# Where four query transposes and four residual tiles are asked for, in a two-block linear-attention and gated-MLP kernel

## The chip, the cores and the metric

The kernel runs on one core of a Trainium2 chip. The metric is the device time of one execution in microseconds (us). The engines are TensorE (PE in the profile, with PEld for its weight loads), VectorE (DVE), ScalarE (ACT), GpSimd (POOL) and SyncE (SP). SP computes nothing here; it issues most of the DMAs, in the order of its queue.

## The reference, cut to what matters

The input `x` has 2048 rows of 1024 numbers. Four layers follow one another, each on the normalised rows and each added to `x`:

```
x = x + A(layernorm(x)); x = x + B(layernorm(x))
x = x + A(layernorm(x)); x = x + B(layernorm(x))

A:  q, k, v = split(x @ wqkv)          # 32 heads of 32
    pq, pk  = phi(q), phi(k)           # phi(t) = t + 1 if t > 0 else exp(t), + 1e-6
    kv = sum_s pk v ;  z = sum_s pk
    o  = (pq @ kv) / (pq . z + 1e-6) ;  return o @ wo
B:  gate, up = x @ W_gate, x @ W_up    # 1024 -> 3584
    return (relu(gate) * up) @ W_down
```

## The kernel before, in words

Rows are held as 16 tiles of 128 rows (`t` = 0 to 15); four tiles make a quarter. The residual lives in SBUF as 16 tiles `x[t]`. Layers 0 and 2 are attention layers (`layer_A`), layers 1 and 3 gated layers (`layer_B`).

**Attention layer, its end.** The queries of a tile, `pq`, are multiplied with the key sums on POOL (`z_mult`, L616), summed on DVE (`z_sum`, L621 to L623), scaled on POOL (`z_scale`, L628), and turned by a DMA transpose that SP issues (L633) into `pqT` of their quarter. The attention's output is then a product of `pqT` with a folded weight `T` (`out_unit`, L659), two units for each tile, added to the residual on DVE (L670 for tiles 0 to 7, L674 for tiles 8 to 15). Quarters 0, 1 and 2 go through `out_unit`. The last quarter (`sc` = 3, tiles 12 to 15) does not: its output is made later, inside the next gated layer, by `out_pairs`, a Strassen-like scheme that first forms sums of `T` (`sums_T`, DVE L505, and in layer 0 also ACT copies of the residual, L697), then sums of `pqT[3]` (`sums_q`, DVE L505), then seven products (L727) that are added to `x[12]` to `x[15]` (L720).

The residual tiles are not kept whole in SBUF in that stretch: in layer 0 they are loaded again from the input (`load_x`, L415, 256 KB each), in layer 2 brought back from a spill (`bring_back`, L256, 512 KB each). `behind(last_turn, ...)` queues these loads on SP behind the last transpose of queries issued so far.

**Gated layer, its start.** Tiles are normalised on ACT and DVE into `xnb` and turned by SP's DMA transposes (`ln_turn`, L378) into `xnT`. For each of the first four pairs of tiles DVE forms four sums (`sums_x`, L893 to L896) into the tiles `s`. A gated unit (`glu`) is 14 products of four matmuls each (L920). The first unit begins with four products that read `xnT` of the first quarter only (`xg`, `xu`, twice), then goes to products that read `s` (`vg`, `vu`, `yg` and so on), for which all four `sums_x` of the chunk are needed. Weights of the units come through a ring of five buffers: `ring.load_to` at the beginning of a unit asks for those of the units ahead (L844 and, where precomputed sums are read back, L847).

**What sets the order.** Work that accompanies the products is handed to a list of due times: `later.at(n, f)` calls `f` after `n` ticks, and every product unit makes one tick. One out unit is one tick, one product of a gated unit is one tick. Inside the attention layer's end DVE and POOL keep exactly the order in which the program asks; the other engines and all of the gated layer are ordered by the framework's planner, which goes by program order and its own costs. All 8 KB-per-partition buffers (weights, `pq`, `pqT`, `xnT`, `s`, and others) share one pool of 16; a new one takes a buffer that has been given back.

The due times around the change, counted from where `run(row_major(out_unit, 1))` starts: `z_scale` of tile 12 is due at tick 3, of 13 at 6, of 14 at 9, of 15 at 12. Residual tiles 8 and 9 are asked for at tick 2, 10 and 11 at 4, 12 and 13 at 6, 14 and 15 at 8. The transposes of `xnT` tiles 4 to 7 are due at 5, 7, 9, 11, `sums_x` at 11, 13, 15 and 16. The first gated unit begins after tick 16.

Of the kernel before, what the change touches and what calls it, by code (L numbers as in the profile page):

```python
# [14 lines left out]
P = 128  # L15
NW = 512
HD = 32
QT = 4
# [71 lines left out]
class _Net:  # L90
# [337 lines left out]
    def layer_A(self, l, last_ln):  # L428
        nc, G, KT, D = self.nc, self.G, self.KT, self.D
        ring, later = self.ring, self.later  # L430
        H = D // NW
        heads = lambda a: a.rearrange("p (h d) -> p h d", d=HD)
        pq_of, pqT, T = {}, {}, []
# [180 lines left out]
        def z_mult(sc, j):  # L614
            prod = ksum
            nc.gpsimd.tensor_tensor(out=prod, in0=pq_of[sc, j], in1=zrow, op=ALU.mult)  # L616
            later.at(2, lambda: z_sum(prod, sc, j))

        def z_sum(prod, sc, j):
            den = self.small.tile([P, D // HD], F32, tag="den")  # L620
            nc.vector.tensor_reduce(out=den, in_=heads(prod), axis=mybir.AxisListType.X, op=ALU.add)  # L621
            nc.vector.tensor_scalar(out=den, in0=den, scalar1=1e-6 * self.mean, scalar2=None, op0=ALU.add)
            nc.vector.reciprocal(out=den, in_=den)  # L623
            later.at(2, lambda: z_scale(den, sc, j))

        def z_scale(den, sc, j):
            pq = pq_of[sc, j]
            nc.gpsimd.tensor_tensor(  # L628
                out=heads(pq), in0=heads(pq),
                in1=den[:, :].unsqueeze(2).to_broadcast([P, D // HD, HD]), op=ALU.mult)  # L630
            if sc not in pqT:
                pqT[sc] = self.slot(f"pqT{l}_{sc}")
            self.last_turn = nc.sync.dma_start_transpose(out=pqT[sc][:, :, j * P:(j + 1) * P], in_=pq)  # L633

        def fold_wo(n):

            n2, a = divmod(n, H)
            if n2 == 0:
                T.append(self.slot(f"T{l}_{a}", [P, 4, D]))
            ps = [pool.tile([P, NW], F32, tag=tag, name=f"fold{l}_{n}_{i}") for i, (pool, tag) in  # L640
                  enumerate(((self.kvp, "kv0"), (self.kvp, "kv1"), (self.ps3, "b"), (self.ps3, "b")))]
            wo = ring.get((l, f"o{n2}"))
            for b in range(R):
                g = a * R + b
                for i in range(R):
                    e = slice(i * HD, (i + 1) * HD)
                    nc.tensor.matmul(ps[i][b * HD:(b + 1) * HD, :], lhsT=kvT[e, g, e],
                                     rhs=wo[e, g, :], start=True, stop=True,
                                     tile_position=(i * HD, b * HD))
            for i in range(R):  # L650
                g = a * R + i
                dst = T[g // 4][:, g % 4, n2 * NW:(n2 + 1) * NW]
                nc.scalar.activation(out=dst, in_=ps[i], func=ACT.Copy)
# [84 lines left out]
        def column_major(f, q):  # L738
            return [lambda j=j, c=c: f(q, j, c) for c in range(H) for j in range(QT)]

        def row_major(f, q):
            return [lambda j=j, c=c: f(q, j, c) for j in range(QT) for c in range(H)]

        def run(*lists):

            n = max(len(u) for u in lists)
            for i in range(n):
                for u in lists:
                    if i < len(u):
                        u[i]()  # L750
                        later.tick()
# [32 lines left out]
        with self.tc.manual_schedule(engines={mybir.EngineType.DVE, mybir.EngineType.Pool}):  # L784
            q3 = row_major(q_unit, self.NQ - 1)
            out0 = column_major(out_unit, 0)
            bring = self.bring_back if l else self.load_x
            ring.load_to(ring.index((l, "v1")) + 1)
            m_products(q3.pop(0))
            q3.insert(0, lambda: None)  # L790
            later.at(1, lambda: self.behind(ring.last, bring, range(self.NS)))
            for t in range(self.NS, self.ST, 2):
                later.at(10 + t, lambda t=t: self.behind(self.last_turn, bring, (t, t + 1)))

            def with_fold(u, i):
                return lambda: (u(), fold_wo(i // 2) if i % 2 == 0 else None)

            run(q3[:2])
            run([with_fold(u, i) for i, u in enumerate(q3[2:] + out0[:1])])
            run(out0[1:3])  # L800
            ring.free_slowly((l, "o0"), later, 2)
            for i in range(11, self.ST):
                later.at(1 + 3 * (i - 11), lambda i=i: z_mult(*divmod(i, QT)))
            self.ln_later(last_ln, 0, 2, 2, 2)
            run(out0[3:])
            for sc in range(1, self.NQ - 1):
                if sc == 1:
                    for j in range(QT):
                        self.ln_at(2 * j + 2, last_ln, QT + j, 2)
                        later.at((11, 13, 15, 16)[j], lambda j=j: self.sums_x(last_ln, 0, j))  # L810
                if sc == 2 and l == 0:
                    for n, w in enumerate("gu"):
                        later.at(2 + 2 * n, lambda w=w: self.make_gu(ring.get((last_ln, 0, w, 0)), w, 0))
                run(row_major(out_unit, sc))
            self.pairs = out_pairs(self.NQ - 1)
# [343 lines left out]
```

## Time and profile before

| what | value |
|---|---|
| median of 4 runs | 1472.87 us |
| the runs | 1474.16, 1471.57, 1474.73, 1471.00 us |
| profiled execution, its own time | 1474.16 us |
| its span in the profile | 1472.4 us |
| mean granted TensorE clock | 0.999 |
| PE, DVE, ACT, POOL busy | 99%, 57%, 39%, 19% of the span |
| transposes of queries on SP (L633) | 32, median 3.6 us from issue to landing |
| transposes of `xnb` (L378) | 32, median 3.9 us from issue to landing |
| bring-back of a residual tile (L256) | 16, 512 KB each, median 6.8 us to landing |

A row of the timeline reads: start and duration in us, engine, line, operation, out<-in, count, and in brackets the idle time of the engine before it with what ended it. `SPq` is SP's queue. Of matmuls, ends overlap, so the distance of starts is what one costs: four matmuls of 128x512 begin 0.86 us after the four before them.

The first attention-to-gated passage lies at 165 to 262 us of the span (layers 0 and 1), the second at 895 to 1000 us (layers 2 and 3). The first gated unit begins at 215.25 us and at 944.29 us.

### The profile page before, as it was taken

The page shows a single profiled execution, that of the slowest core. Times are in us where ns is not written, and L with a number is a line of the kernel's source. Part 1 is how long each engine was busy: PE and PEld are TensorE (multiplying, and loading weights), DVE is VectorE, ACT ScalarE, POOL GpSimd, SP SyncE. Part 2 cuts the span into 40 slices and gives each one's busy share as a digit, 9 for nine tenths or more (in the row PEclk, how much of TensorE's full clock was granted, in tenths as well). Part 3 has the DMA queues.
Part 4 walks back from the last instruction along what each step waited for, and adds up shares of the span by engine and source line. Part 5 has one row for each costly group of instructions (what it writes and reads, how often), then busy time and mean ns, then how long its engine had stood idle before and what let it go on. Part 6 is the DMA issues. An engine that isn't in the chain of part 4 may idle for free.

```text
span 1472.4 us, 18695 instructions
## 1 busy us (share of the span) xinstructions
PE 1461.9 (99%) x6959; PEld 663.5 (45%) x6959; DVE 840.9 (57%) x1483; ACT 579.1 (39%) x1027; POOL 285.9 (19%) x190
## 2 busy tenths in 40 slices
PE   9999999999999999999999999999999999999999
PEld 4444444444444444444444444444444444444444
DVE  7968688666684544455368565666345433443632
ACT  6872574333340333340077626533333203333300
POOL 1444851011100011110024476310111001111000
PEclk9999999999999999999999999999999999999999
DMA  9940794564559944446843029955444687444461
GB/s 282 240 151 12 185 244 163 183 218 165 202 174 259 344 147 144 143 147 185 262 87 71 1 37 290 278 176 193 144 143 150 181 250 254 145 147 150 149 204 43
DMA packets 318363, 255.51 MB, mean 174 GB/s; under 512 B 105792, under 2 KB 291392, under 8 KB 317376
## 3 DMA queue, kind: packets, MB, share of 16 engines
q1 hardware_dynamic: 308304, 234.00, 54.1%
q10 hardware_dynamic: 9968, 20.32, 3.6%
q8 instruction: 54, 0.88, 0.2%
q14 instruction: 37, 0.30, 0.1%
HBM read 195.04 MB, written 34.60 MB: 156 GB/s over the span
## 4 chain that ended last, share of the span: by engine, by line
PE 93%; DVE 3%; ACT 1%; DMA 1%; POOL 1%; issue 1%; SPq 0%; DVEq 0%; POOLq 0%; ACTq 0%
PE ps L454 14%; PE dy L1019 10%; PE yg L920 10%; PE yu L920 10%; PE dx L1019 7%; PE dv L1019 7%; PE xg L920 6%; PE xu L920 6%; PE zu L920 3%; PE zg L920 3%; PE vu L920 3%; PE vg L920 3%; PE my L538 3%; PE ps L659 3%; PE mv L538 2%; PE mx L538 2%
## 5 line engine op out<-in xcount | busy, mean ns | idle before, releaser
L920 PEld LDWEIGHTS <-w 128*128 128x128 f16 (+1 forms) x3136 | 307.1, 98 | 377.3 <-issue 8.4
L973 POOL TENSOR_TENSOR h<-m5u,m5g 128x512 f16<-128x512 f32 x56 | 71.2, 1271 | 817.1 <-DVE m5u L969 773.3
L454 PE MATMUL ps<-w,xnT 128*128 128x512 bf16 x1024 | 223.4, 379 | 0.2 <-ACT xnT L322 0.2
L1019 PEld LDWEIGHTS <-h 128*128 128x128 f16 x1120 | 109.6, 98 | 132.1
L454 PEld LDWEIGHTS <-xnT 128*128 128x128 bf16 x1024 | 99.4, 98 | 120.0 <-issue 1.4
L956 DVE TENSOR_TENSOR zg<-yg,m5g 128x512 f32<-128x512 f32 x56 | 39.1, 699 | 190.9 <-PE yg L920 190.9
L920 PE MATMUL yg<-s,w 128*128 128x512 f16 x448 | 115.8, 381 | 0.5 <-DVE zg L956 0.5
L920 PE MATMUL xu<-xnT,w 128*128 128x512 f16 x448 | 115.0, 379 | 1.0 <-DVE x L674 1.0
L920 PE MATMUL yu<-s,w 128*128 128x512 f16 x448 | 115.2, 379 | 0.1
L920 PE MATMUL xg<-xnT,w 128*128 128x512 f16 x448 | 115.1, 379 | 0.0
L928 ACT ACTIVATE m5g<-m5g 128x512 f32<-128x512 f32 x56 | 35.2, 629 | 194.4 <-DVE m5g L969 194.4
L1019 PE MATMUL dy<-w,h 128*128 128x512 f16 x448 | 98.0, 379 | 0.0
L1019 PE MATMUL dx<-w,h 128*128 128x512 bf16 x448 | 97.3, 379 | 0.0
L401 ACT ACTIVATE e<-e,eps 128x512 f32<-128x512 f32 x128 | 92.4, 722 | 4.2
L400 ACT ACTIVATE e<-ps 128x512 f32<-128x512 f32 x128 | 76.0, 594 | 45.8 <-PE ps L454 44.3
L616 POOL TENSOR_TENSOR kvc<-pq,kvc 128x1024 f32<-128x1024 bf16 x32 | 73.5, 2298 | 60.3 <-DVE den L621 35.0
L659 PE MATMUL ps<-T,pqT 128*128 128x512 bf16 x384 | 83.6, 379 | 0.0
L937 ACT ACTIVATE m5g<-vg 128x512 f32<-128x512 f32 x56 | 33.4, 597 | 112.9 <-PE vg L920 88.5
L473 POOL TENSOR_TENSOR kvc<-kvc,slab 128x512 f32<-128x512 f32 x46 | 58.6, 1280 | 74.3 <-DVE slab L404 59.1
L931 DVE TENSOR_TENSOR h<-yu,r 128x512 f16<-128x512 f32 x56 | 38.7, 691 | 57.7 <-PE yu L920 57.7
L969 DVE TENSOR_TENSOR m5u<-yu,m5u 128x512 f32<-128x512 f32 x56 | 38.7, 691 | 53.6 <-PE yu L920 53.6
L1019 PEld LDWEIGHTS <-e 128*128 128x128 f16 x448 | 43.8, 98 | 52.9
(154 smaller groups left out, 1964.9 us busy)
## 6 DMA issues: line engine op xcount, KB each, us to landing
w<-in_B_W_gate_dram SPq DMA_DIRECT2D x56, 512.0 KB, 5.7
w<-in_B_W_up_dram SPq DMA_DIRECT2D x56, 512.0 KB, 4.9
w<-td SPq DMA_DIRECT2D x32, 896.0 KB, 4.7
w<-in_B_W_down_dram SPq DMA_DIRECT2D x24, 896.0 KB, 5.2
w<-tg SPq DMA_DIRECT2D x42, 512.0 KB, 6.9
w<-tu SPq DMA_DIRECT2D x42, 512.0 KB, 5.7
w<-in_A_wqkv_dram SPq DMA_DIRECT2D x10, 1024.0 KB, 7.2
away<-x SPq DMA_DIRECT2D x16, 512.0 KB, 4.2
```

Source lines behind the costliest of these rows:

```text
L400: nc.scalar.activation(out=e, in_=ps, func=ACT.Relu, scale=-1.0)
L401: nc.scalar.activation(out=e, in_=e, func=ACT.Exp, scale=-1.0, bias=self.eps6[:, 0:1])
L454: nc.tensor.matmul(by_row(ps), lhsT=self.xnT[l, l_q][:, kt, j * P:(j + 1) * P], rhs=w[:, kt, :].rearrange("p (b i d) -> p i b d", i=R, d=H ...
L473: nc.gpsimd.tensor_tensor(out=ksum[:, cols], in0=ksum[:, cols], in1=pk, op=ALU.add)
L538: nc.tensor.matmul(banks[j], lhsT=A(i)[:, j * P:(j + 1) * P], rhs=B(i), start=start and i == 0, stop=i == NS - 1, skip_group_check=True)
L616: nc.gpsimd.tensor_tensor(out=prod, in0=pq_of[sc, j], in1=zrow, op=ALU.mult)
L659: nc.tensor.matmul(ps, lhsT=pqT[sc][:, g, j * P:(j + 1) * P], rhs=T[g // 4][:, g % 4, n2 * NW:(n2 + 1) * NW], start=(g == 0), stop=(g == G ...
L920: nc.tensor.matmul(ps, lhsT=W[w][m][:, k, :], rhs=A[m][:, k, :], start=start and k == 0, stop=k == 3, skip_group_check=True)
L931: self.last_put = nc.vector.tensor_tensor(out=h[:, b, :], in0=ps, in1=R.pop(b), op=ALU.mult)
L956: nc.vector.tensor_tensor(out=Z[w], in0=Y[w], in1=V[w], op=ALU.add)
L973: nc.gpsimd.tensor_tensor(out=h[:, 3, :], in0=V["u"], in1=V["g"], op=ALU.mult)
L1019: nc.tensor.matmul(banks[j], lhsT=A(k)[:, j * P:(j + 1) * P], rhs=w[:, i, :], start=start and k == 0, stop=k == self.U - 1, skip_group_che ...
```

## The change

The four transposes of the last quarter's queries are taken out of `z_scale` and issued by a function of their own, `q_turn`. Quarters 0 to 2 call it from `z_scale` as before. For the last quarter it is due 11 to 14 ticks after the start of the third quarter's eight out units, which is ticks 3 to 6 of the first gated unit. Residual tiles 12 to 15 are taken out of the loop that asks for tiles 8 to 15 in pairs, and asked for one each at ticks 7 to 10 of the first gated unit, behind the last transpose. The buffer of `pqT[3]` is taken where the first of the transposes is asked for.

```
@@ z_scale
             nc.gpsimd.tensor_tensor(
                 out=heads(pq), in0=heads(pq),
                 in1=den[:, :].unsqueeze(2).to_broadcast([P, D // HD, HD]), op=ALU.mult)
+            if sc < self.NQ - 1:
+                q_turn(sc, j)
+
+        def q_turn(sc, j):
             if sc not in pqT:
                 pqT[sc] = self.slot(f"pqT{l}_{sc}")
-            self.last_turn = nc.sync.dma_start_transpose(out=pqT[sc][:, :, j * P:(j + 1) * P], in_=pq)
+            self.last_turn = nc.sync.dma_start_transpose(out=pqT[sc][:, :, j * P:(j + 1) * P],
+                                                         in_=pq_of[sc, j])
@@ layer_A
-            for t in range(self.NS, self.ST, 2):
+            for t in range(self.NS, self.ST - QT, 2):
                 later.at(10 + t, lambda t=t: self.behind(self.last_turn, bring, (t, t + 1)))
@@ layer_A, for sc in range(1, self.NQ - 1)
+                if sc == 2:
+                    for j in range(QT):
+                        later.at(11 + j, lambda j=j: q_turn(self.NQ - 1, j))
+                    for t in range(self.ST - QT, self.ST):
+                        later.at(3 + t, lambda t=t: self.behind(self.last_turn, bring, (t,)))
```

## The prediction

> **What bounds the kernel now.** I read the page first: TensorE is busy for nearly the whole span, so only its idle time and its clock can be gained, and anything else costs time only by making it wait.
>
> ```profile
> PE 1461.9 (99%) x6959; PEld 663.5 (45%) x6959; DVE 840.9 (57%) x1483; ACT 579.1 (39%) x1027; POOL 285.9 (19%) x190
> ```
>
> Next the waits of PE over the whole span (us in total, times, longest). There are few, and the largest is one of 2.7 us.
>
> ```profile
> PE vg L920 <- DVE s L893: 2.9, 2, 2.7
> PE idle L272 <- DVE e L269: 1.3, 1, 1.3
> PE xu L920 <- DVE x L674: 1.0, 1, 1.0
> ...
> PE yg L920 <- DVE zg L956: 0.5, 2, 0.3
> ```
>
> Then the timeline of PE at the start of layer 3's first unit. The reader is to see the idle 2.70 us in front of `vg`, and that the products behind it start 1.49 and 1.71 us apart, where 0.86 is the rule.
>
> ```profile
> 946.88 1.03 PE L920 MATMUL xu<-xnT,w 128*128 128x512 f16 x4
> 950.61 1.02 PE L920 MATMUL vg<-s,w 128*128 128x512 f16 x4 [2.70 <-DVE s L893]
> 951.47 1.70 PE L920 MATMUL vu<-s,w 128*128 128x512 f16 x4
> 952.96 1.91 PE L920 MATMUL yg<-s,w 128*128 128x512 f16 x4
> 954.67 1.24 PE L920 MATMUL yu<-s,w 128*128 128x512 f16 x4
> ```
>
> The table by stretches says why: the column behind the POOL's is the granted clock, 0.51 in 951.6 to 955.1, and 1.00 around it.
>
> ```profile
> 951.60:955.10 3.50, 3.50 (x11) 1.22 (x9) 0.71 (x2) 1.19 (x2) 0.00 (x0) 0.51 1.06 349
> ```
>
> Last, what `s` waited for: DVE's and SP's timelines. DVE stands idle for 2.97 us until a transpose of `xnb` (L378) lands. SP issues that one at 942.87, behind the brought-back tiles (L256) and query transposes (L633).
>
> ```profile
> 947.98 0.42 DVE L893 TENSOR_TENSOR s<-xnT 128x512 f16<-128x512 f16 x1 [2.97 <-DMA xnT<-xnb]
> ```
>
> ```profile
> 925.73 3.17 SPq L633 DMA_TRANSPOSE pqT<-pq  x1
> ...
> 931.38 0.60 SPq L256 DMA_DIRECT2D x<-away  x1
> ...
> 934.67 0.58 SPq L256 DMA_DIRECT2D x<-away  x1
> 935.35 1.52 SPq L633 DMA_TRANSPOSE pqT<-pq  x1
> 936.97 3.35 SPq L378 DMA_TRANSPOSE xnT<-xnb  x2
> 940.37 1.06 SPq L256 DMA_DIRECT2D x<-away  x2
> 941.53 1.23 SPq L633 DMA_TRANSPOSE pqT<-pq  x1
> 942.87 4.46 SPq L378 DMA_TRANSPOSE xnT<-xnb  x2
> 947.42 1.29 SPq L633 DMA_TRANSPOSE pqT<-pq  x1
> ```
>
> The order of the rows gives the tiles: the L633 shown are the queries of tiles 12, 13, 14 and 15, the L256 rows tiles 12 to 15, and the two L378 at 942.87 are tiles 6 and 7. ACT had finished their `xnb` at 935.7 and 937.8 (rows L214 at 934.51 for 1.23 and 936.52 for 1.24). So about 7 us pass between ready and issued.
>
> **The change part by part, layer 3.** Ahead of tiles 6 and 7 SP loses three query transposes (3.17, 1.52, 1.23 us of issue) and four bring-backs (0.60, 0.58, 1.06): 8.16 us of its queue, and from the DMA engines four transfers of 512 KB, which at the 301 GB/s of 930 to 945 us are 7.0 us, and three transposes at about 1.3 us (two neighbours landed 1.3 us apart), 3.9 us. Tile 7 then goes out when it is ready and its predecessor has been issued: 937.8, plus at most one issue of 1.3 us, 939.1. With the landing times of the L378 in that stretch (3.2 to 5.8 us) it is there at 942.3 to 944.9; today it lands at 949.4. What is late next is DVE: between the sums stand L674 rows that wait for PE's last out units. The last of these units ends at about 944.4, DVE adds it in 0.68 and forms the first of tile 7's sums in 0.42, and with the sums of tile 6 in front (1.5 us) `s` is ready at 945.0 to 946.0. PE reaches `vg` at 947.9. Margin some 2 us, so the wait of 2.70 goes whole.
>
> The clock. The stretch at 0.51 lies right behind that wait and is the only one below 1.00 among those I looked at around the two passages. Its loss by rows: from `vg` at 950.61 to `yg` at 955.74 are four starts, 5.13 us, against 4 x 0.864 = 3.46, so 1.67; or 3.5 x 0.49 = 1.7. If the wait goes, I take this with it. Sum for layer 3: 2.70 + 1.7 = 4.4 us.
>
> [...]
>
> **Layer 1** (205 to 230 us). SP loses the same rows, with 256 KB tiles. The waits of PE there are 1.0 (`xu` on L674), 0.25 (`vg` on `s`) and 0.5 (`yg` on `zg`). DVE shows no idle time over 0.15 us from 206 to 224 us: it is behind by its own work (a weight sum L856 takes 2.01 there, 0.43 elsewhere), and its order is written out and not changed. So earlier transposes buy nothing: 0, with 1.25 as the upper bound. Below, a loss is bounded by the rival.
>
> **What is moved in.** Four transposes (1.23 to 2.12 us of issue) and four loads now stand in the first unit. *SP:* behind them wait the ring's loads of the units ahead. In layer 3 those asked for earlier (L844/L847 at 948.80 and 950.08) now follow tile 7 and are earlier by some 8 us. Those of 951.59 and 954.83 come behind the moved block: 4 x 1.3 + 4 x 0.6 = 7.6 us of issue, but starting from about 943, so at 951 to 955 again. The transfers moved (7.0 + 4 x 1.3 = 12.2 us) are the same bytes in another order; today's landings were 961.9 and 965.0, the first need is the third unit, about 973 less 4.4: margin 6 us. *POOL:* the scaling L628 stays; SP no longer waits for it at these rows (window 925 to 950: 2.4 us, counted in the rows above). *DVE:* `sums_q` reads `pqT[3]` at 974.68 and 247.18; the moved transposes land by about 955 and 225. Margin 15 us or more. *ACT:* in layer 0 the copies L697 start at 234.38 and read tiles 12 to 15. SP reaches these at about 211.7 + 1.5 (two ring loads) + 4 x 1.5 + 4 x 0.5 = 221, landing 3 to 7 us later (L415 lands after 3.1 us here, after 6.0 in the median), by 228. Margin 6 us. In layer 2 the tiles are first needed at 988.76 (L720). *Buffers:* `pqT[3]` takes its buffer later; at that time the third quarter's `pqT` and `kvc` have been given back, so none is missing. All 0, while these margins last.
>
> **Sum.** Against the profiled execution: 1474.16 - 4.4 = 1469.8. The median is 1.29 lower than that execution. The other runs may lose less in this place, which their times don't tell; on the median the gain lies between 2.70 and 4.4, so 1470.2 to 1468.5. I take **1469.0**, nearer the full sum as the profile shows it whole.
>
> A measurement of this kernel can tell about 0.2% from no change, 2.9 us: below 1469.9 is faster, above 1475.8 slower.
>
> **The rivals.**
>
> *The hole is filled (0.22).* SP's free time goes to the ring's loads of 948.80 and 950.08 (2 MB, 7 us at 301 GB/s), which the planner may draw ahead of tiles 6 and 7, now that one buffer more is free. Tile 7 would land at up to 944.9 + 7, where it lands today. For: the DMA engines are full in this stretch. Against: in the profile these loads stand behind everything that is asked for before them, though SP waited now and then. Gain 0 to 2.7: about 1472.
>
> *The change does not do what it says (within the same 0.22).* The moved transposes are ready early, and the planner might issue them nearly where they were; then nothing changes: 1472.9.
>
> *Slower (0.22).* In layer 1 SP stands from 220.91 to 230.43 before a ring load that waits for a buffer. If the planner sets the moved transposes or the loads of tiles 12 to 15 behind it, the tiles go out at 231 to 238 and land 3 to 7 us later, at 234 to 245. ACT's copies L697 then hold ACT's queue from 234.38 on, up to 8 us, with PE's evictions behind them, and the half clock adds 1.7. It decides once tile 15 lands after about 238. For: the planner reorders, and 16 buffers are nearly all taken there. Against: that ring load belongs to a later unit and is asked for later. Price up to 9.7, less the 4.4: +5, about 1478.
>
> **How the numbers follow.** Forecast 0.56, filled hole or no change 0.22, slower 0.22. The forecast's own range is 1467.2 (layer 1's 1.25 go too) to 1470.2. The range reaches from 1466.5 into the slower case, to 1476.5, leaving out about 2 in 10. Faster 0.56 (a few of the forecast fall short of 0.2%, as many of the rival's reach it), same 0.22, slower 0.22.
>
> **What would show it.** Right: in layer 3 the L378 of tiles 6 and 7 issued by 940, `s` ready before PE asks, no wait of `vg` on L893, clock 1.00 throughout; L633 and L256 of tiles 12 to 15 after the first unit began. Layer 1's wait of 1.0 unchanged. Wrong: a new wait of PE in the first three units of either gated layer, on a weight, on ACT behind L697 or on `pqT`; or L844 in front of the L378 of tile 7.

## The result, and the profile after

The changed kernel takes 1474.16 us (median of 38 runs, 1471.62 to 1476.9), the kernel before 1471.85 us (58 runs, 1470.14 to 1477.53). The ratio, as the record estimates it from all runs, is 1.001, 95% interval 1.0006 to 1.0015 (the medians alone give 1.0016). The forecast was 1469.0 and faster; it became a little slower, by less than the 0.2% that the prediction had set for telling a change. The profiled execution of the changed kernel took 1476.12 us, its span is 1474.3.

PE, DVE, ACT and POOL have the same instructions in the same order in both kernels. Only SP's queue differs, so every difference below comes from when a DMA was issued or landed. Lines past the change have moved: the ring's loads are L854 (L844 before), DVE's weight sums L864 to L867 (L854 to L857), the moved transposes L637 (L633), `zg` L966 (L956).

PE's row of waits in the changed kernel's profile (us in total, times, longest):

```profile
PE yg L930 <- DVE zg L966: 3.5, 2, 3.3
...
PE xu L930 <- DVE x L679: 1.0, 1, 1.0
...
PE vg L930 <- DVE s L903: 0.2, 1, 0.2
```

The wait of 2.7 us on `s` is gone, as forecast. A wait of 3.3 us on `zg` has come. In the timeline of PE it lies in the first passage, in the second gated unit of layer 1:

```profile
236.60 1.03 PE L930 MATMUL vg<-s,w 128*128 128x512 f16 x4
237.46 0.59 PE L930 MATMUL vu<-s,w 128*128 128x512 f16 x2
241.33 1.87 PE L930 MATMUL yg<-s,w 128*128 128x512 f16 x4 [3.27 <-DVE zg L966]
242.99 1.91 PE L930 MATMUL zg<-s,w 128*128 128x512 f16 x4
```

The products behind it are again 1.7 us apart, and the table by stretches has the granted clock (the figure behind POOL's) at 0.50 there:

```profile
240.60:247.30 6.70, 5.97 (x15) 2.05 (x15) 3.60 (x6) 2.58 (x5) 0.00 (x0) 0.50 0.19 78
247.30:252.00 4.70, 4.70 (x23) 2.15 (x22) 3.00 (x5) 2.35 (x5) 1.27 (x1) 0.99 0.28 82
```

DVE's timeline says what `zg` waited for. DVE had to form the sums of the third unit's weights first, and their up weights had not landed. `zg` stands behind them in the same queue, after three sums of `T`:

```profile
231.44 0.68 DVE L864 TENSOR_TENSOR w<-w 128x1024 f16<-128x1024 bf16 x1
235.11 0.69 DVE L864 TENSOR_TENSOR w<-w 128x1024 f16<-128x1024 bf16 x1 [2.99 <-DMA w<-in_B_W_up_dram]
...
240.59 0.69 DVE L966 TENSOR_TENSOR zg<-yg,m5g 128x512 f32<-128x512 f32 x1
```

And SP's timeline says why. The ring's loads for the second unit's up and the third unit's gate weights stand at 210.86 and 211.48, then the moved block (the four transposes L637 and the four tiles L415), then at 227.40 the third unit's up weights:

```profile
210.86 0.53 SPq L854 DMA_DIRECT2D w<-in_B_W_up_dram  x1
211.48 0.60 SPq L854 DMA_DIRECT2D w<-in_B_W_gate_dram  x1
212.17 12.12 SPq L637 DMA_TRANSPOSE pqT<-pq  x4
224.34 2.96 SPq L415 DMA_DIRECT2D x<-in_A_x_dram  x4
227.40 0.43 SPq L854 DMA_DIRECT2D w<-in_B_W_up_dram  x1
```

Before the change that load was issued at 215.58 and landed at 224.7, DVE's two sums L854 followed each other without idle time, and PE waited 0.19 us (SP's, DVE's and PE's timelines of the kernel before):

```profile
214.91 0.57 SPq L844 DMA_DIRECT2D w<-in_B_W_gate_dram  x1
215.58 2.13 SPq L844 DMA_DIRECT2D w<-in_B_W_up_dram  x1
...
231.12 1.28 DVE L854 TENSOR_TENSOR w<-w 128x1024 f16<-128x1024 bf16 x2
...
237.93 1.02 PE L920 MATMUL yg<-s,w 128*128 128x512 f16 x4 [0.19 <-DVE zg L956]
```

Now the load is issued 11.8 us later and lands at 235.1.

The second passage went as forecast. PE runs from `xu` into `vg` at its normal distance of 0.86:

```profile
953.24 1.03 PE L930 MATMUL xu<-xnT,w 128*128 128x512 f16 x4
954.10 1.03 PE L930 MATMUL vg<-s,w 128*128 128x512 f16 x4
954.97 1.03 PE L930 MATMUL vu<-s,w 128*128 128x512 f16 x4
```

The two profiled executions add up. The first unit of layer 1 began at 215.25 before and 215.56 after, that of layer 3 at 944.29 and 950.65: 6.05 us lost between them. Of these 3.27 - 0.19 = 3.08 are the wait on `zg`. The clock is at half for 6.83 us from 240.52, of which 6.02 lie behind the wait's end: 3.0 more. From layer 3's first unit to the end the changed kernel gains 6.36 - 1.96 (the difference of the spans) = 4.4, the 2.70 and 1.7 of the forecast. The two waits alone, 2.70 gone and 3.08 come, nearly cancel: in the 10 of 39 executions of the changed kernel whose mean clock is 1.000 the median is 1472.0, close to the 1471.85 of the kernel before. So most of the loss seems to be half clock, which came in 29 of the 39; that is argued from runs of several chips, not shown by itself.

### The profile page after: what moved, and what is told of

Same layout as the page of the kernel before. It is cut to its first block, busy times and chain, and to the rows that moved or that the text cites. A ratio compares the mean times of both kernels' runs of the same rounds, so it can differ in the third digit from the quotient of the medians.

```text
span 1474.3 us, 18702 instructions
## 1 busy us (share of the span) xinstructions
PE 1463.1 (99%) x6959; PEld 663.7 (45%) x6959; DVE 842.0 (57%) x1483; ACT 579.5 (39%) x1027; POOL 285.8 (19%) x190
## 4 chain that ended last, share of the span: by engine, by line
PE 92%; DVE 2%; ACT 2%; DMA 1%; SPq 1%; POOL 1%; issue 1%; DVEq 0%; POOLq 0%; ACTq 0%
PE ps L454 14%; PE dy L1029 10%; PE yu L930 10%; PE yg L930 10%; PE dx L1029 7%; PE dv L1029 7%; PE xg L930 6%; PE xu L930 6%; PE zu L930 3%; PE zg L930 3%; PE vu L930 3%; PE vg L930 3%; PE ps L664 3%; PE my L538 3%; PE mv L538 2%; PE mx L538 2%
## 5 line engine op out<-in xcount | busy, mean ns | idle before, releaser
L966 DVE TENSOR_TENSOR zg<-yg,m5g 128x512 f32<-128x512 f32 x56 | 39.1, 699 | 190.9 <-PE yg L930 190.9
L938 ACT ACTIVATE r<-yg 128x512 f32<-128x512 f32 x56 | 33.4, 597 | 89.5 <-PE yg L930 89.5
```

Source lines behind the costliest of these rows:

```text
L938: self.last_relu = nc.scalar.activation(out=out, in_=ps, func=ACT.Relu)
L966: nc.vector.tensor_tensor(out=Z[w], in0=Y[w], in1=V[w], op=ALU.add)
```

## The experiments

All edits below are against the changed kernel unless said otherwise, and in all of them only SP's queue differs from the kernel before. Ratios are to runs of the kernel before on the same chip. The first four share their runs of before (median 1473.59), the last three were on another chip and share others (1472.17), so times are to be compared within a group only.

**The second passage alone.** The move is made in layer 2 only:

```
-            if sc < self.NQ - 1:
+            if sc < self.NQ - 1 or l not in (2,):
                 q_turn(sc, j)
...
-            for t in range(self.NS, self.ST - QT, 2):
+            for t in range(self.NS, self.ST - (QT if l in (2,) else 0), 2):
...
-                if sc == 2:
+                if sc == 2 and l in (2,):
```

> Transposes and tiles are moved in layer 2 only; layer 0 asks for them as before the change. Theory (late weights): the change gains its 2.7 us in the second passage and loses them in the first, where the moved block holds back the ring's load that DVE's weight sums of the third unit read. Then here the first passage is as before (no wait of PE on zg over 0.3 us), vg has no wait in the second, the time is 2.7 us under before's runs with full clock: about 1468.7, ratio 0.998. Rival (the gain is not there, because before's wait on vg was an accident of the one profiled execution): within 0.5 us of before.

Measured: 1470.33 us, ratio 0.997 (0.9958 to 0.9982). PE's waits over 0.3 us that are left are those of the kernel's beginning, the 1.0 of `xu` in layer 1, which the change never touched, and one of 1.0 on a load of the first layer, 0.5 in the changed kernel's own profile:

```profile
PE idle L272 <- DVE e L269: 1.3, 1, 1.3
PE xu L931 <- DVE x L679: 1.0, 1, 1.0
PE ps L454 <- DMA w<-in_A_wqkv_dram: 1.0, 1, 1.0
PE tp L312 <- DVE x L170: 0.7, 1, 0.7
PE yg L931 <- DVE zg L967: 0.5, 2, 0.3
PE vg L931 <- DVE s L904: 0.2, 1, 0.2
```

So the gain is real. Between the medians it is 3.3 us, within the 2.70 to 4.4 of the forecast. It was lost elsewhere.

**The first passage alone.** The same edit with `(0,)` for `(2,)`.

> Transposes and tiles are moved in layer 0 only. Theory (late weights): both waits of PE are there, 3.3 us on zg in the first passage and 2.7 on vg in the second, each with or without a stretch at half clock; 1474.5 with full clock, median 1476 to 1477.5, ratio 1.003. Rival (the loss comes from elsewhere, for instance from the tiles brought back late in layer 2): as before, 1471.9.

Measured: 1478.44 us, ratio 1.0029 (1.0021 to 1.0038). The ratio is the expected one; the time is a little over the expected one, as this chip's runs of the kernel before are. In all 11 runs the mean clock is below 1.000. Both waits of PE are there:

```profile
PE vg L931 <- DVE s L904: 3.2, 2, 3.0
PE yg L931 <- DVE zg L967: 3.1, 2, 2.8
```

**The weights first.** The whole change stays; the first unit of layer 1 asks for one ring load more, so that the third unit's up weights come before the moved block:

```
-                ring.load_to(ring.index((l, c, "g", u)) + 5)
+                ring.load_to(ring.index((l, c, "g", u)) + (6 if first and u == 0 else 5))
```

> The whole change, but the first unit of layer 1 asks for one ring load more (six instead of five), so that the up weights of the third unit stand ahead of the moved transposes on SP. Theory (place in the queue): that load lands by about 222 instead of 235.1, DVE's L864 waits for nothing, PE's 3.3 us on zg go, the second passage keeps its gain: 1468.7, ratio 0.998, as with layer 2 alone. Rival (the DMA engines are full, and whatever is asked for there lands late): it lands after 229 all the same, and PE still waits 1 us or more.

Measured: 1469.60 us, ratio 0.9972 (0.996 to 0.9983). In SP's timeline the third of the loads L854 now precedes the moved block:

```profile
210.08 0.53 SPq L854 DMA_DIRECT2D w<-in_B_W_up_dram  x1
210.71 0.59 SPq L854 DMA_DIRECT2D w<-in_B_W_gate_dram  x1
211.35 2.88 SPq L854 DMA_DIRECT2D w<-in_B_W_up_dram  x1
214.34 10.89 SPq L637 DMA_TRANSPOSE pqT<-pq  x4
225.28 2.56 SPq L415 DMA_DIRECT2D x<-in_A_x_dram  x4
```

It lands at 221.4, and in PE's timeline the wait on `zg` is back at its size of before:

```profile
237.48 1.02 PE L930 MATMUL yg<-s,w 128*128 128x512 f16 x4 [0.20 <-DVE zg L966]
```

The moved block still takes 13.5 us of SP's queue (15.1 in the changed kernel), and the DMA engines carry the same bytes. What cost the time was the one load behind it.

**In layer 0 the transposes alone.** Layer 2 as changed; in layer 0 the tiles are asked for as before the change:

```
-            for t in range(self.NS, self.ST - QT, 2):
+            for t in range(self.NS, self.ST - (QT if l in (2,) else 0), 2):
...
+                if sc == 2 and l in (2,):
                     for t in range(self.ST - QT, self.ST):
```

> Layer 2 as changed; in layer 0 the transposes are moved and the tiles are asked for as before the change. The moved transposes took 12.1 us of SP's queue in front of the ring's load, the tiles 3.0. Theory (the sum of both makes it late by 3.3): with the tiles gone the load is issued 3.0 earlier, at 224.4, and lands at about 232; DVE asks for it at 231.7, so 0 to 0.5 us of PE's wait are left: 1468.7 to 1469.3. Rival (the transposes alone are enough): PE waits 2 us or more on zg, 1471 to 1473.

Measured: 1471.15 us, ratio 0.9982 (0.9972 to 0.9991). The load is issued at 224.91, half a microsecond later than expected, and lands at 232.6. In PE's timeline the wait is 1.64, between the two expectations and nearer the rival's:

```profile
238.88 1.02 PE L931 MATMUL yg<-s,w 128*128 128x512 f16 x4 [1.64 <-DVE zg L967]
```

The expectation took the end of the transposes from the changed kernel. Here, with the tiles' 1 MB asked for before them, the four took 13.46 us of issue instead of 12.12 (SP's timeline of this kernel):

```profile
211.35 13.46 SPq L637 DMA_TRANSPOSE pqT<-pq  x4
224.91 1.65 SPq L855 DMA_DIRECT2D w<-in_B_W_up_dram  x1
```

**In layer 0 the tiles alone.** The counterpart: transposes of layer 0 as before the change, tiles moved in both layers.

```
-            if sc < self.NQ - 1:
+            if sc < self.NQ - 1 or l not in (2,):
                 q_turn(sc, j)
...
+                if sc == 2 and l in (2,):
                     for j in range(QT):
```

> Layer 2 as changed. In layer 0 only the tiles are moved. Theory (late weights by place in the queue): the third unit's up weights stand behind four tile loads but no transposes, are issued at about 218 and land by 227, before DVE asks at 231: no wait of PE on zg over 0.3 us, ratio 0.997. Rival (any load put in front of the weights in this stretch is enough): PE waits 1 us or more on zg, ratio 0.998 to 0.999.

Measured: 1469.81 us, ratio 0.9987 (0.9978 to 0.9996). The load is issued at 220.43, 2.4 us later than expected, since a pair of tile loads in front of it took 4.80 us to issue (SP's timeline of this kernel):

```profile
215.53 4.80 SPq L415 DMA_DIRECT2D x<-in_A_x_dram  x2
220.43 0.38 SPq L855 DMA_DIRECT2D w<-in_B_W_up_dram  x1
```

It lands at 228.1, still before DVE asks, and PE's wait is 0.19. The ratio is nearer the rival's, but on this chip the other two kernels, whose layer 0 is unchanged, have 0.9984, so it shows no loss; the wait decides. So it is the transposes that exhaust the margin; the tiles make it worse.

Over these kernels the wait on DMA passes through DVE to PE almost unchanged. The columns are DVE's wait on the up weights and PE's wait on `zg` behind it, in us:

| kernel | load issued | landed | DVE waits | PE waits |
|---|---|---|---|---|
| before | 215.58 | 224.7 | 0 | 0.19 |
| the weights first | 211.35 | 221.4 | 0 | 0.20 |
| in layer 0 the tiles alone | 220.43 | 228.1 | 0 | 0.19 |
| in layer 0 the transposes alone | 224.91 | 232.6 | 1.36 | 1.64 |
| the first passage alone | 226.34 | 233.8 | 2.56 | 2.8 |
| the changed kernel | 227.40 | 235.1 | 2.99 | 3.27 |

**In layer 2 the transposes alone, and the tiles alone.** Layer 0 is as before the change in both; the edits are those above with the conditions exchanged (`(2,)` for the part that is moved, `()` for the part that is not).

> Layer 0 as before the change. In layer 2 only the transposes are moved; tiles 12 to 15 are asked for where they were. Theory (both share the backlog ahead of tiles 6 and 7: 5.9 us of SP's queue by the transposes, 2.2 by the tiles; 3.9 and 7.0 us of transfers): the transposes of tile 7 are issued when its xnb is ready, but the brought-back tiles still fill the DMA engines; tile 7 lands 3 to 5 us earlier than before, and the wait of vg (2.7 us) goes, or less than 0.5 is left: ratio 0.997 to 0.9985. Rival (the 2 MB of tiles are what makes it late): 1.5 us or more of the wait are left.

> Layer 0 as before the change. In layer 2 only the tiles are moved; the transposes are issued where they were. Theory (both share the backlog): SP loses 2.2 us of issue and the DMA engines 7.0 us of transfers ahead of tile 7, issues shorten as the backlog goes; tile 7 lands 3 us or more earlier, and of the wait of 2.7 us less than 0.5 is left: ratio 0.997 to 0.9985. Rival (SP's queue and its waits for the scaling are what makes it late, not the transfers): 1 us or more of the wait is left, ratio 0.9985 to 1.

Measured: 1469.68 us, ratio 0.9984 (0.9975 to 0.9993), for the transposes, and 1469.69 us, ratio 0.9984 (0.9976 to 0.9993), for the tiles. Either part alone removes the wait on `s`: the last `xnb` transpose lands at 945.5 and 943.5 instead of 949.4. With the transposes alone DVE still waits 0.98 us for the tile before it; with the tiles alone it waits for none. So both shared the backlog, and moving either was enough.

The transposes moved alone show a small price that the forecast had put at nothing. In DVE's timeline `sT` waits for a transpose of `pq`:

```profile
958.08 1.23 DVE L505 TENSOR_TENSOR sT<-T 128x2048 f16<-128x2048 bf16 x1 [0.76 <-DMA pqT<-pq]
```

`sT` needs a buffer of the pool, and it got one that the late transposes give back. That is inferred from the wait alone and not shown. PE waited 0.9 us for `zg` behind it.

**Faster than both.** All of these kernels but the first passage alone are faster than the kernel before, by 0.1 to 0.3%, with intervals that lie below 1, while the changed kernel's lies above. The five of them in which no wait on `zg` or `s` over 1 us is left have medians of 1469.6 to 1470.3 us, too close to each other to be ranked by these runs.

## Why the prediction was wrong

What failed is a term that the prediction put at nothing: SP's queue in "What is moved in". In the profiled executions it cost 3.08 us of waiting and 3.0 us of half clock in layer 1. By the prediction's own steps:

- *Layer 3, the wait of 2.70 us goes.* Right. The prediction had tile 7 issued by 939.1 and landed at 942.3 to 944.9. Put on the time scale of the kernel before (the first unit began 6.36 us later) it was issued at 937.8 and landed at 940.9, earlier still; `vg` found its sums ready 1.5 us early, where 2 were forecast.
- *The clock, 1.7 us.* Right for the profiled execution, too much for the median. Among the 48 runs of the kernel before beside the experiments 17 have a mean granted clock below 1.000 (to three places), with a median of 1473.94 against 1472.01 for the other 31. So about one run in three lost it, and not evenly: 13 of 21 on one chip and 4 of 27 on the other. Why the chips differ is open.
- *Layer 1, the waits of 1.0, 0.25 and 0.5 stay.* Right for the first two; the third grew to 3.5.
- *What is moved in: SP, "the first need is the third unit, ... margin 6 us".* This step failed. It followed the ring's loads behind the moved block in layer 3 only, and took PE's products as their first reader. In layer 1 their first reader is DVE: the weight sums of the third unit are due in the second unit, and before the change read the load at 231.7, 7 us after it landed. In DVE's timeline this wait, which ends at 235.11, stands in front of `zg` at 240.59.
- *The size of the block.* The prediction put it at 4 x 1.5 + 4 x 0.5 = 8 us in layer 1. It took 15.1: two of the transposes needed 5.16 and 4.12 us to issue, where 1.23 had been the commonest. With 8 us the load would have gone out at about 221 and landed, by the issue-to-landing time of 7.7 seen here, at 229, before DVE asked; with the tiles alone it did go out at 220.43, landed at 228.1, and PE did not wait longer. So either error alone was enough to hide the loss: with the right reader and a block of 8 us the load still seemed in time, and with a block of 15.1 and PE as the reader too. In layer 3, where the prediction had 7.6 us, the block took 11.3 (948.46 to 959.72), and the margin there held.
- *ACT, tiles 12 to 15 in time for the copies.* Right: the last landed at 233.3, the copies began at 237.7, delayed by the same stall.
- *Buffers, none is missing.* Held for PE in the changed kernel; not quite in the experiment with the transposes alone.

Of the rivals, "the hole is filled" did not happen: the ring's loads stayed behind tile 7. The slower rival had the right place, SP's queue in layer 1 and the ring's loads, and the wrong order: it set the moved block behind a load that waits, and what happened was a load behind the moved block.

## What to carry to other kernels

When DMAs are moved to a later place, list every transfer that is queued behind the new place, and for each its first reader on any engine, not only on the engine that uses it in the end; a helper that prepares the data can be due a whole unit earlier. Do it for each place where the code runs: the same lines, here with 256 KB tiles and weight sums in one layer and with 512 KB tiles and stored sums in the other, gained 4.4 us at one place and lost 6.1 at the other in the profiled executions. The repair was cheap here: one load asked for ahead of the moved block kept the whole gain.

## What the runs showed of the hardware

The half clock came with waits of PE. In two profiles its stretch is on record: 3.41 us in the kernel before (951.67 to 955.08), which begins 1.06 us after the end of a wait of 2.70, and 6.83 in the changed kernel (240.52 to 247.35), which begins 2.46 us into a wait of 3.27. The length of the wait does not tell it alone. With the first passage alone PE waited 2.8 us on `zg` and 3.0 on `vg`, and the mean clock of that profile is 0.999 over 1474.9 us. By my estimate from these two, under 0.0015 of the span is lost, which is at most 4.4 us of half clock for the two waits; so one of them came with less than the 3.41 of the wait of 2.70. With the transposes alone in layer 0 the wait was 1.64 and the mean clock 1.000. What else decides was not shown. Of the other runs only the mean clock is on record, not the waits. It was below 1.000 in 17 of 48 runs of the kernel before, in 29 of 39 of the changed kernel (its profiled execution among them), in all 11 with both waits (the first passage alone), in 1 of 9 of the transposes alone in layer 0 (1.64 us in the profile), and in 3 of 45 of the five kernels whose profiles have no wait over 1.3 us.

The issue of a transpose on SP was no fixed cost here: rows of 1.23 us and of 5.16 us stand for the same instruction. In the changed kernel's table by stretches the DMA engines' share is 0.56 at 205.0 to 212.2 us, where two transposes of `xnb` took 1.23 us each to issue, and 1.19 at 212.2 to 224.3, where the four moved ones took 5.16, 1.30, 4.12 and 1.26. That the long issues come from a backlog in the DMA engines fits, and was not tried by itself.
